# One transformer block on one core: a shared pool of PSUM banks in the projections, a split projection in the last attention unit, and late tokens normalised a step ahead

## The chip, the cores and the metric

The kernel runs on one core of a Trainium2 chip. Its engines are TensorE (PE, with its weight loads shown as PEld), VectorE (DVE), ScalarE (ACT), GpSimd (POOL) and SyncE (SP, which here issues nearly all DMAs). Products land in PSUM, eight banks of 512 fp32 columns on 128 partitions. The metric is the device time of one execution in microseconds, as the median over several runs. Smaller is better.

## What is computed

One pre-norm transformer block on 2048 tokens of width 640, in fp32: attention with 32 heads of 20, then a gated feed-forward part of width 1728.

```python
x = A_x                                            # 1 x 2048 x 640
qkv = (layernorm(x) @ A_wqkv).reshape(B, S, 3, 32, 20)
p = softmax(einsum("bhqd,bhkd->bhqk", q, k) * 20 ** -0.5)
h = x + einsum("bhqk,bhkd->bhqd", p, v).reshape(B, S, D) @ A_wo
z = layernorm(h)
out = h + (silu(z @ B_w_gate) * (z @ B_w_up)) @ B_w_down
```

## The kernel before

All 128-wide operands are split into a high and a low fp32r part, so that a product of two of them is three matmuls (high x high, high x low, low x high). The order of all instructions is written out by hand: each engine runs its own queue in the order in which the program emits it, and waits come from the dependences between tiles.

**First stage: queries, keys and values** (from line 704). The tokens come in four chunks of 512. A chunk is loaded, normalised (`norm`, L714; the normalisation itself is `apply`, L719), turned by TensorE (`flip`, L739, by 64-row halves) and split into `z_hi` and `z_lo`. The list `work` (L888 to 895) holds the projections: 40 *blocks* (128 queries or keys x 512 tokens) and 32 *values* (128 tokens x 320 columns). Each is a *sum* of 15 products of 128 rows; all but the first two blocks run as 30 products of 64 rows, first the 15 of rows 0 to 63 (half 0), then, into the same bank, the 15 of rows 64 to 127 (half 1). Products of different halves can run at the same time in the two halves of the array.

In between, TensorE makes part of the row maxima that the softmax needs later. `max_differences` (L192) is one product in each half for a pair of heads, into two banks: ACT takes a Relu of one half of the columns (L197) and DVE a maximum with the rest (L199). `max_twice` (L205) works in one half of the rows: a first product, whose Relu ACT writes to SBUF (L222), and later a `second` product, with which DVE makes the maximum (L216). The queues `early` (240 entries, groups 1 to 7 and one unit of group 0) and `others` (48 entries of group 0) hold these steps; `next_pair` (L507) takes from one or the other, and a step is usable only when its staged keys and queries have landed and are ready. Keys are staged in places that `raw_place` and `place` (L363 to 372) prepare.

The order is made by a planner that runs while the program is emitted, the class `Halves` (L514, object `pe`). It keeps a model clock for each half (`t`), the time at which each engine is free (`free`, moved by `use`) and the time at which PSUM banks are free. There are two sets of banks: three for sums (`ones`, L525) and five for maxima and turns (`single`, L523). `pair` (L583) issues a step of the maxima if the two oldest of the five banks are free by the model; a `max_twice` takes both of them from its first product on, and its second bank stays marked as taken until `finish_second` (L639) has issued the second product. `run` (L650) starts a sum when one of the three banks is free, and then alternates between the halves by their model clocks; `issue` (L547) emits one product; `may_follow` (L572) says whether half 1 of the oldest sum may run. `before_flip` (L616) waits in model time for two banks. `finish` and `drain` (L674, L681) complete sums and maxima at the end.

PSUM is opened three times: a pool for the first turns (`psum_f`, L70), closed at L869; a second for the rest of the stage (`psum`, L871), closed at L991; and one for attention (`psum_a`, L995: four `ps_one`, three `ps_max`, one `acc`). After attention a fourth (`psum2`, L1494) has four `ps_b` and four `ps_a`.

**Attention** (loop at L1417). 32 units (8 groups of 4 heads x 4 chunks of queries), each with 16 slots, one for 128 keys. In a slot TensorE makes four score products (`scores`, L1331, 62 rows each), ACT four exponentials (L1342), and `weigh` (L1344) multiplies the probabilities of the slot before with the values, in four 32-column tiles, into the bank `acc`. The remaining maxima (`max_one`, L224, and DVE's L235) are placed between the scores by the strings in `ORDER`. Without maxima left the slot is `"sSsSW"`, where W is the weighing and whatever hangs on it: one step from the list `extra`, among others. In the last two units `extra` is the output projection of a finished chunk of tokens (`projection`, L1038): eight steps `first` (`project`, 15 matmuls of 128 rows x 320 columns, L1070, then on DVE the addition L1076 and the statistics L1077), three of normalisation, and four turns (`flip`, L1095), each of which copies and splits its result with `split` (high part by ACT at L88, low part by DVE at L89).

**Feed-forward** (from L1494). The last two chunks are projected, and chunks 2 and 3 are normalised, turned, combined and stored for later in small steps, one in each step of the first products (`late_tokens`, L1831 on: `apply` L1859 makes a normalised tile in one of two buffers, `flip` L1874 turns it with L1878). Then the gate and up products (`ps_a`, L1514), and the down products (`ps_b`, L1608) follow, whose results DVE adds to `h` (L1613); the last row of tokens is stored by L1672.

## Time and profile before

| | us |
|---|---|
| median of 3 runs | 2040.0 |
| lowest and highest of them | 2034.8, 2041.55 |
| the profiled execution, its own time | 2035.66 |
| its span, first to last instruction | 2033.9 |
| mean granted clock of TensorE in it | 0.997 |

The stages, by the trace: the first exponential of attention starts at 328.69, the last unit's slots run from about 1418 to 1468, and the last product ends at 2030.

How to read the rows. In the view of busy time by stretches a row has the stretch, its length, and then for PE, weight load, DVE, ACT and POOL the busy us and, in brackets, the instructions; then the granted clock of TensorE (1.00 is full), the busy share of the DMA engines, and GB/s. A group by line has line, engine, operation, tile written <- tiles read, shapes and count, then busy us and mean ns of one, then the idle time of the engine just before them. In the view of one line the three numbers after a count are the shortest, median and longest duration in ns, and the two after them the first and last start. A row of the timeline has start, duration, engine, line, operation, and in square brackets the idle time before it and what ended it; consecutive equal instructions are merged. A row of the waits has who waited, for whom, us in total, how often, and the longest. The busy time of PE is modelled and overlaps, so the rate at which products start says more than the busy share.

### The profile page before, as it was taken

The page shows a single profiled execution, that of the slowest core. Times are in us where ns is not written, and L with a number is a line of the kernel's source. Part 1 is how long each engine was busy: PE and PEld are TensorE (multiplying, and loading weights), DVE is VectorE, ACT ScalarE, POOL GpSimd, SP SyncE. Part 2 cuts the span into 40 slices and gives each one's busy share as a digit, 9 for nine tenths or more (in the row PEclk, how much of TensorE's full clock was granted, in tenths as well). Part 3 has the DMA queues.
Part 4 walks back from the last instruction along what each step waited for, and adds up shares of the span by engine and source line. Part 5 has one row for each costly group of instructions (what it writes and reads, how often), then busy time and mean ns, then how long its engine had stood idle before and what let it go on. Part 6 is the DMA issues. An engine that isn't in the chain of part 4 may idle for free. (4 is left out here: it accounts for less than half of the span.)

```text
span 2033.9 us, 39129 instructions
## 1 busy us (share of the span) xinstructions
PE 2008.8 (99%) x13716; PEld 1238.9 (61%) x13716; DVE 1612.6 (79%) x3241; ACT 1462.4 (72%) x2952; POOL 785.7 (39%) x1079
## 2 busy tenths in 40 slices
PE   7999999999999999999999999999999999999999
PEld 6899996333333333333333333345598888888888
DVE  6678788888888888888888888885377666676677
ACT  3788988999999999999999999987633222211221
POOL 5554450334434334344430011011145454744555
PEclk9999999999999999999999999999999999999999
DMA  7776663343443534444433123211158654974642
GB/s 227 243 222 186 203 185 100 113 128 99 150 124 113 163 123 138 129 141 146 141 126 109 30 65 80 83 62 49 41 193 292 222 193 156 346 272 159 202 151 95
DMA packets 205124, 305.03 MB, mean 150 GB/s; under 512 B 47664, under 2 KB 82480, under 8 KB 203904
## 3 DMA queue, kind: packets, MB, share of 16 engines
q1 hardware_dynamic: 204832, 302.53, 45.9%
q8 instruction: 109, 1.79, 0.4%
q14 instruction: 87, 0.71, 0.1%
q10 hardware_dynamic: 96, 0.00, 0.0%
HBM read 205.78 MB, written 95.68 MB: 148 GB/s over the span
## 5 line engine op out<-in xcount | busy, mean ns | idle before, releaser
L1342 ACT ACTIVATE probs<-ps_one 128x512 f32<-128x512 f32 x2048 | 1056.9, 615 | 62.0 <-PE ps_one L1336 24.2
L235 DVE TENSOR_REDUCE mx<-ps_max 128x1 f32<-128x512 f32 x1472 | 925.4, 684 | 116.2 <-PE ps_max L229 64.1
L1336 PE MATMUL ps_one<-q_stk,k_stk 62*128 62x512 f32 x2048 | 583.5, 431 | 1.2 <-DVE mx L199 1.2
L1346 PE MATMUL acc<-probs,v_stk 128*32 128x512 f32 x4096 | 546.7, 605 | 0.0
L229 PE MATMUL ps_max<-k_stk,q_stk 60*128 60x512 f32 x1472 | 488.7, 440 | 0.1
L1336 PEld LDWEIGHTS ps_one<-q_stk,k_stk 62*128 62x128 f32 x2048 | 290.5, 185 | 284.7 <-ACT probs L1342 269.7
L229 PEld LDWEIGHTS ps_max<-k_stk,q_stk 60*128 60x128 f32 x1472 | 245.2, 185 | 165.4 <-DVE mx L235 126.9
L1729 DVE TENSOR_TENSOR tmp<-ps_a,tmp 128x512 f32<-128x512 f32 x208 | 141.3, 690 | 122.1 <-PE ps_a L1514 96.4
L1346 PEld LDWEIGHTS acc<-probs,v_stk 128*32 128x32 f32 x4096 | 80.6, 108 | 181.7 <-issue 169.5
L1608 PE MATMUL ps_b<-halves,yp 128*128 128x320 f32 x1032 | 179.0, 308 | 1.5 <-POOL yp L89 1.3
L1608 PEld LDWEIGHTS ps_b<-halves,yp 128*128 128x128 f32 x1032 | 165.2, 188 | 17.5 <-POOL yp L89 1.5
L1514 PE MATMUL ps_a<-t,units 128*128 128x512 f32 x624 | 162.5, 396 | 0.0
L246 POOL CAST both<-neg 128x16 fp32r<-128x16 f32 x32 | 6.6, 207 | 361.6 <-PE ps_one L1336 153.7
L1514 PE MATMUL ps_a<-z,units 128*128 128x512 f32 x516 | 133.9, 394 | 0.0
L89 POOL TENSOR_TENSOR yp<-y,yp 128x256 fp32r<-128x256 f32 x96 | 60.2, 627 | 189.8 <-ACT yp L88 189.8
L1514 PEld LDWEIGHTS ps_a<-t,units 128*128 128x128 f32 x624 | 112.6, 188 | 18.5
L1613 DVE TENSOR_TENSOR h<-ps_b,h 128x320 f32<-128x320 f32 x248 | 110.0, 482 | 6.9 <-PE ps_b L1608 5.4
L216 DVE CUSTOM_DVE_ANT_0 q_stk<-ps_single,q_stk 128x512 f32<-128x512 f32 x143 | 95.7, 689 | 22.4 <-ACT q_stk L222 15.0
L1514 PEld LDWEIGHTS ps_a<-z,units 128*128 128x128 f32 x516 | 93.1, 187 | 16.0
L556 PE MATMUL ps_one<-z_hi,w_hi 64*128 64x512 f32 x380 | 99.1, 402 | 1.8 <-ACT z_hi L88 1.7
L88 ACT ACTIVATE yp<-tmp 128x512 fp32r<-128x512 f32 x40 | 25.3, 632 | 103.2 <-POOL tmp L1601 103.2
L1381 POOL TENSOR_TENSOR o<-o,rb 128x512 f32<-128x512 f32 x31 | 39.9, 1286 | 152.9 <-ACT probs L1342 55.8
(221 smaller groups left out, 3017.9 us busy)
## 6 DMA issues: line engine op xcount, KB each, us to landing
units<-w_d SPq DMA_DIRECT2D x186, 256.0 KB
w_d<-stage SPq DMA_DIRECT2D x106, 256.0 KB
halves<-j_d SPq DMA_DIRECT2D x70, 320.0 KB
k_stk<-qk_d SPq DMA_DIRECT2D x112, 160.0 KB
j_d<-stage SPq DMA_DIRECT2D x42, 320.0 KB
q_stk<-qk_d SPq DMA_DIRECT2D x64, 160.0 KB
k_stk<-qk_d SPq DMA_DIRECT2D x112, 80.0 KB
rb<-r_d SPq DMA_DIRECT2D x32, 256.0 KB
```

The source lines that it names most:

```text
L89: lo_engine.tensor_tensor(out=lo, in0=src, in1=hi.bitcast(F32), op=ALU.subtract)
L216: nc.vector.tensor_tensor_reduce(out=place, in0=pss[1], in1=place, scale=1.0, scalar=LEAST, op0=ALU.add, op1=ALU.max, accum_out=mx[:, b, p ...
L229: nc.tensor.matmul(ps, queries[u][rows, pair, t * P : (t + 1) * P], keys[u // NC][rows, pair, kc * CH : (kc + 1) * CH], start=True, stop=True,
L235: nc.vector.tensor_reduce(mxs[u][:, b, pair, t, kc : kc + 1], ps, axis=AX.X, op=ALU.max)
L556: product = nc.tensor.matmul(job["ps"][:, :out], lhs, rhs, start=(half == 0 and i == 0), stop=(half == 1 and i == job["n"] - 1),)
L1336: nc.tensor.matmul(ps, keys[u // NC][rows, p, kt * P : (kt + 1) * P], queries[u][rows, p, :], start=True, stop=True,)
L1342: nc.scalar.activation(probs[p][:, b, :], ps, AF.Exp, scale=scale)
L1346: nc.tensor.matmul(acc[32 * j : 32 * j + 32, :], values[u // NC][:, kt, j * VW : j * VW + 32], probs[j // 2][:, j % 2, :], start=(kt == 0) ...
L1514: nc.tensor.matmul(ps.rearrange("p (t n) -> p t n", t=TPC), w[k][:, i], z[k][:, :, j], start=(first and m == 0), stop=(last and m == len(n ...
L1608: nc.tensor.matmul(ps, a, b, start=(n == 0), stop=(n == len(pairs) - 1))
L1613: nc.vector.tensor_tensor(out=h, in0=ps, in1=h, op=ALU.add)
L1729: add = lambda out, ps, x: nc.vector.tensor_tensor(out=out, in0=ps, in1=x, op=ALU.add)
```

## The change

**PSUM.** One pool with one tile of eight banks serves the whole kernel. The names `ps_wide`, `ps_one`, `ps_max`, `ps_b` and `bank` now return slices of it by turns. Nothing is closed and opened again. For attention the planner's four oldest banks become `ps_one`, the next three `ps_max`, the last `acc`.

**Planner.** There is one table of eight banks, `places`. `banks(n)` gives the n oldest if they are free by the model. A sum takes one when it starts, and any number of sums may be open. A `max_twice` takes one bank for its first product, and another only when the second product is issued. `others` goes first whenever it holds more than a quarter as many entries as `early`. `before_flip` issues products of half 1 while it waits, and two assertions become `finish_before`, which completes older sums.

```diff
+BEHIND = 2
+SHARE = 4
...
+    psum = ctx.enter_context(tc.tile_pool(name="psum", bufs=1, space=bass.MemoryType.PSUM))
+    banks = psum.tile([P, 8, CH], F32, name="banks")
+    wide_places, one_places = [2, 4, 6], []
+
+    def turn(places):
+
+        places.append(places.pop(0))
+        return places[-1]
...
     def ps_one():
-        return psum.tile([P, CH], F32, name="ps_one", tag="ps_one", bufs=ones)
...
+        return banks[:, turn(one_places) if one_places else pe.take()]
...
-        def second():
-            product(pss[1], first)
+        def second(at):
+            ps, = ps_at(at)
+            product(ps, first)
...
         def next_pair():
             load_items()
-            queues = (others, early) if slot[0] >= begins(NC - 1) else (early, others)
+            first = slot[0] >= begins(NC - 1) or len(others) * SHARE > len(early)
+            queues = (others, early) if first else (early, others)
...
-                self.single = [[0.0] for _ in range(5)]
+                self.places = dict.fromkeys(range(8), 0.0)
...
+            def oldest(self):
+                return sorted(self.places, key=self.places.get)
+
             def banks(self, n):
-                return all(
-                    at[0] is not None and at[0] + MARGIN <= self.now() for at in self.single[:n]
-                )
+                places = self.oldest()[:n]
+                return places if self.places[places[-1]] + MARGIN <= self.now() else None
...
             def pair(self):
                 t = self.now()
-                if not self.banks(2):
+                if not self.banks(1):
                     return False
...
+                at = self.banks(1 if half is not None else 2)
+                if at is None:
+                    return False
+                second = queue.pop(ahead)[1](at)
                 if half is not None:
                     start = self.stream(half, 0.231)
-                    del self.single[:2]
                     seen = self.use("scalar", 0.48, start + 0.43) + 0.2
-                    bank = [None]
-                    self.single += [[seen], bank]
-                    self.second[half] = second, seen, bank
+                    self.places[at[0]] = seen
+                    self.second[half] = second, seen
                     return True
...
+            def finish_before(self, c):
+                while any(job["c"] < c for job in self.jobs):
+                    if self.may_follow():
                         self.issue(1)
                         self.pair()
                     else:
                         self.rest()
+
+            def finish_second(self, half):
+                if not self.second[half]:
+                    return False
+                second, seen = self.second[half]
+                at = self.banks(1)
+                if at is None or self.now() + 0.43 < seen:
+                    return False
+                self.second[half] = None
+                second(at)
+                start = self.stream(half, 0.231)
+                self.places[at[0]] = self.use("vector", 0.62, max(seen, start + 0.43)) + 0.14
+                return True
...
+                while not self.banks(1):
+                    if not self.finish_second(1) and self.may_follow():
+                        self.issue(1)
+                        self.pair()
+                    else:
+                        self.rest()
+                job["place"], = self.banks(1)
+                self.places[job["place"]] = math.inf
...
+    places = pe.oldest()
+    one_places, max_places, acc_place = places[:4], places[4:7], places[7]
```

**Smaller edits of the first stage.** The raw places are filled by an ACT copy instead of two small DMAs; chunk 1 is normalised on DVE instead of POOL, and the planner's price for POOL's goes from 1.3 to 2.55.

```diff
         def raw_place():
-            return place(raw_tile().rearrange("p a b -> p (a b)")[:, : 2 * CH])
...
+            return place(raw_tile().rearrange("p a b -> p (a b)")[:, : 2 * CH], nc.scalar)
...
+            if engine is nc.scalar:
+                some = w_hi.rearrange("p k c -> p (k c)")[:, : 2 * CH].bitcast(F32)
+                nc.scalar.activation(t, some, AF.Copy)
+                pe.use("scalar", 1.0)
+                return t.rearrange("p (h n) -> p h n", h=2)
...
-                (nc.gpsimd if c else nc.vector).tensor_scalar(
+                (nc.gpsimd if c > 1 else nc.vector).tensor_scalar(
...
-                + [(("pool", 1.3), lambda t=t: apply(t), c) for t in range(TPC)]
+                + [
+                    (("pool", 2.55) if c > 1 else ("vector", 0.75), lambda t=t: apply(t), c)
+                    for t in range(TPC)
+                ]
```

**Attention.** The first slot has no maxima. In the last unit W weighs two slots at once in every even slot and none in the odd ones, up to the last. The projection that runs there (of chunk 1) is made in two halves of 64 rows into two banks, the second two products behind the first, and added by two DVE operations; its turns leave the high part to DVE too.

```diff
+            rows = [slice(b * ROW, (b + 1) * ROW) for b in range(2)] if halved else [slice(0, P)]
+            pss = [ps_of() for _ in rows]
+            terms = ((o_hi, wo_hi), (o_hi, wo_lo), (o_lo, wo_hi))
+            for n in range(3 * ND + BEHIND * (len(rows) - 1)):
+                for i, (r, ps) in enumerate(zip(rows, pss)):
+                    m = n - BEHIND * i
+                    if 0 <= m < 3 * ND:
+                        (a, w), k = terms[m // ND], m % ND
+                        nc.tensor.matmul(
+                            ps[:, :HALF], a[r, k, :], w[r, k, hs],
+                            start=(m == 0), stop=(m == 3 * ND - 1),
+                        )
             h = h_c[c][:, t, hs]
-            nc.vector.tensor_tensor(out=h, in0=ps[:, :HALF], in1=h, op=ALU.add)
+            for ps in pss:
+                nc.vector.tensor_tensor(out=h, in0=ps[:, :HALF], in1=h, op=ALU.add)
...
+                if c == 0:
+                    split(src, hi, lo, nc.vector)
+                else:
+                    nc.vector.tensor_copy(hi, src)
+                    nc.vector.tensor_tensor(out=lo, in0=src, in1=hi.bitcast(F32), op=ALU.subtract)
...
-            order = ORDER[now[0] % len(ORDER)] if singles[0] or singles[1] else "sSsSW"
+            order = ORDER[now[0] % len(ORDER)] if now[0] and (singles[0] or singles[1]) else "sSsSW"
...
-                    if todo:
-                        weigh_next()
+                    both = u == NU - 1 and kt < NT - 1
+                    for _ in range(2 * (1 - kt % 2) if both else 1):
+                        if todo:
+                            weigh_next()
```

**Feed-forward.** The late tokens' steps are reordered, so that each tile is normalised a step before it is turned, in five steps for each pair of tiles instead of six; the last row of tokens is stored in two parts.

```diff
+            tt = self.c * TPC + self.t + i
+            first = HALF if tt == NT - 1 else 0
+            if self.fs[0] == NF - 2 and (half == 1 or first):
...
+                cs = slice(first * half, D if half else HALF)
+                nc.sync.dma_start(out[tt * P : (tt + 1) * P, cs], h_c[self.c][:, self.t + i, cs])
...
-        items = moments() + [lambda: apply(2, 0)]
+        items = moments() + [lambda: apply(2, 0), lambda: apply(3, 0)]
         short = len(items)
         items.append(store)
+        items.append(lambda: flip(2, 0))
         for t in range(TPC):
...
+            more = t + 1 < TPC
+            items += [
+                lambda t=t, more=more: (store(), more and apply(2, t + 1), flip(3, t)),
+                lambda t=t, more=more: (store(), sums(t), more and apply(3, t + 1)),
+                lambda t=t, more=more: (store(), more and flip(2, t + 1)),
+                lambda t=t: (store(), keep(zz[2, t], t_d[0], t)),
+                lambda t=t: (store(), keep(zz[3, t], t_d[1], t, nc.vector)),
+            ]
```

171 lines of the change are left out of this document (66 added, 105 removed).

## The prediction

> **What bounds the kernel now.** I read the page first, then busy time by stretches, then the counts by line in the first stage, then the waits and the timeline of the places that the edits touch.
>
> ```profile
> span 2033.9 us, 39129 instructions
> PE 2008.8 (99%) x13716; PEld 1238.9 (61%) x13716; DVE 1612.6 (79%) x3241; ACT 1462.4 (72%) x2952; POOL 785.7 (39%) x1079
> ```
>
> A PE that is 99% busy says little here: in the first 326 us most products use 64 of the 128 rows, and two may run at once, one in each half of the rows. The stretches (time; then busy us and instructions of PE, weight load, DVE, ACT, POOL; granted clock; DMA share; GB/s) show three kinds of stage.
>
> ```profile
> 40.00:80.00 40.00, 36.42 (x336) 33.49 (x335) 18.81 (x79) 25.68 (x67) 24.94 (x17) 0.96 0.73 224
> 49.20:50.80 1.60, 0.03 (x1) 0.00 (x0) 0.00 (x0) 0.00 (x0) 1.60 (x2) 1.00 0.95 223
> 52.40:55.70 3.30, 3.30 (x18) 3.15 (x17) 1.55 (x8) 2.30 (x7) 3.30 (x3) 0.52 0.62 165
> 80.00:320.00 240.00, 238.59 (x2310) 223.04 (x2309) 192.66 (x680) 202.70 (x434) 114.34 (x85) 1.00 0.67 207
> 326.00:328.10 2.10, 0.68 (x2) 0.18 (x1) 2.05 (x12) 1.30 (x5) 0.00 (x0) 1.00 0.48 187
> 328.20:335.70 7.50, 7.50 (x33) 3.29 (x37) 4.92 (x8) 4.93 (x10) 0.00 (x0) 0.54 0.30 92
> 337.00:1360.00 1023.00, 1023.00 (x7190) 401.56 (x7186) 908.75 (x1491) 996.83 (x1968) 313.70 (x526) 1.00 0.36 112
> 1418.00:1452.00 34.00, 34.00 (x227) 21.69 (x219) 10.32 (x28) 20.38 (x40) 5.96 (x4) 1.00 0.19 52
> 1520.00:1560.00 40.00, 37.66 (x199) 32.09 (x198) 30.93 (x62) 16.05 (x33) 22.39 (x21) 1.00 0.80 281
> 1560.00:1760.00 200.00, 200.00 (x1034) 174.18 (x1033) 140.10 (x262) 46.00 (x100) 99.56 (x155) 1.00 0.65 224
> ```
>
> Attention (337 to 1360) is ACT's: 996.83 of 1023 us. The steady feed-forward stage is PE's, without a gap. The change leaves the work of both as it is, so what it can win lies in the first 337 us, in the last unit (1418 to 1470) and around 1520 to 1560.
>
> How full is the first stage? Counts by line, and one price of a stream:
>
> ```profile
> L556 PE MATMUL ps_one<-z_hi,w_hi 64*128 64x512 f32 x380 | 99.1, 402 | 1.8 <-ACT z_hi L88 1.7
> L556 PE MATMUL ps_one<-w_lo,z_hi 64*128 64x320 f32 x320 | 63.4, 308 | 0.0
> L216 DVE DVE_READ_ACCUMULATOR2_ANT mx<- x208: 77/83/88, 133.7 to 321.3; 128x1 f32 x104
> L216 DVE CUSTOM_DVE_ANT_0 q_stk<-ps_single,q_stk x143: 678/691/693, 133.0 to 320.7; 128x512 f32<-128x512 f32 x143
> L199 DVE DVE_READ_ACCUMULATOR2_ANT mx<- x160: 78/83/85, 53.3 to 328.0; 128x1 f32 x160
> 1556.27 2.09 PE ps_a L1514 x9
> 23.97 0.73 PE L556 MATMUL ps_one<-z_hi,w_hi 64*128 64x512 f32 x2
> ```
>
> Nine products of 512 columns in 2.09 us are 0.232 us each; 320 columns are 0.147 (0.73 us for five, in the slot shown below). The sums are three rows like the first (1140 products) and three like the second (960). Each of the 208 accumulator reads of L216 stands for two products, each of the 160 of L199 for one: 576. With both halves always streaming that is (1140 x 0.232 + 960 x 0.147 + 576 x 0.232) / 2 = 270 us; with about 8 for the 120 transposes, 278. It runs from 23.97 to 326: 302 us. **So 24 us, 8%, are lost to one half standing idle, to PE waits and to a halved clock.** That is the most that the edits of this stage can give.
>
> **The change, part by part.**
>
> 1. *Chunk 1 normalised on DVE instead of POOL.*
>
> ```profile
> 39.04 5.00 POOL L720 TENSOR_SCALAR xt<-xt,mv,r_a 128x640 f32<-128x640 f32 x2 [2.05 <-PE ps_one L556]
> 45.27 5.48 POOL L720 TENSOR_SCALAR xt<-xt,mv,r_a 128x640 f32<-128x640 f32 x2
> 50.80 0.27 PE L745 MATMUL ps_single<-ident,xt 64*128 64x64 f32 x2 [1.57 <-POOL xt L720]
> L720 DVE TENSOR_SCALAR xt<-xt,mv,r_a x4: 605/609/611, 11.1 to 12.7; 128x640 f32<-128x640 f32 x4
> ```
>
> Four operations of 2.5 us on POOL end at 50.75; PE's first turn of chunk 1 waits for the last. On DVE they are 4 x 0.61 = 2.4 us, on an engine busy for 18.81 of these 40 us, so the turn finds its input ready. That removes the idle 1.6 us (49.2 to 50.8) and, if the clock is then not halved, half of 3.3 us (52.4 to 55.7): 1.6 + 1.6 = 3.2. What may be late next is the copy and split on ACT, busy 25.68 of 40. The new fill of four raw places (two small DMAs each become one 128x1024 ACT copy; two 512-wide activations of 0.60, L1342's row under part 3, are 1.2 us, 4.8 in all) goes into ACT's 14 idle us there; with that cover gone it costs up to 4.8. The eight DMA issues that go only free SP. I take **-3**, ends -5 and +2.
>
> 2. *One pool of eight banks.* Before, three banks are the sums' and five the pairs' and turns', and a product that has a partner holds two of five from its start. After, any step takes the oldest free bank, a sum may start while a bank is free, and the partner's bank is taken when the partner is issued. No instruction is added to a product. What it can win is the idle half: 24 less the 3.2 of part 1 leaves 21 us. Against all of it speaks ACT, busy 202.70 of 240: were 17 us of that stretch gone it would be at 91%, and its work comes in bursts. The trace has no row for a bank that the planner withheld; the bounds are -17 (all) and +15 (rival D). A quarter, **-4**, is nearest to what ACT leaves between its bursts. The order of the queue (four-to-one between the later groups' products and those of the first) moves products, not their number: 0. The planner's new POOL price of 2.55 matches the rows above; in later chunks no PE wait for POOL's normalisation shows: 0.
>
> 3. *Start of attention.* The scores' first banks now are the four oldest, and the closing of the pool is gone, as are the three maxima of the first slot.
>
> ```profile
> PE ps_one L1336 <- DVE mx L199: 1.2, 1, 1.2
> 328.69 4.03 ACT L1342 ACTIVATE probs<-ps_one 128x512 f32<-128x512 f32 x8 [1.39 <-PE ps_max L229]
> 334.58 0.60 ACT L1342 ACTIVATE probs<-ps_one 128x512 f32<-128x512 f32 x1 [1.86 <-PE ps_one L1336]
> 337.16 2.07 ACT L1342 ACTIVATE probs<-ps_one 128x512 f32<-128x512 f32 x4 [0.18 <-PE ps_max L229]
> ```
>
> PE idles before 328.1 for DVE's last maxima, is then at half clock until 335.7, and ACT loses 1.39 + 1.86 us and some smaller gaps: between 328.69 and 337.16, 8.5 us, it makes twelve exponentials, three slots, worth 3 x 2.07 = 6.2. So 2.3 lie here, plus the 1.2 before it, plus what the earlier start gives. The skipped maxima come back in one slot at the end of their row; a slot with maxima leaves ACT idle for (1023 - 996.83)/1023, under 3% of it: nothing. Ends 0 and -6; **-4**.
>
> 4. *Last unit.* One slot with a projection now:
>
> ```profile
> 1421.03 0.76 PE L1336 MATMUL ps_one<-q_stk,k_stk 62*128 62x512 f32 x4
> 1421.72 1.06 PE L1346 MATMUL acc<-probs,v_stk 128*32 128x512 f32 x8
> 1422.72 1.00 PE L1070 MATMUL ps_max<-wo_hi,o_hi 128*128 128x320 f32 x5
> 1423.56 0.90 PE L1070 MATMUL ps_max<-wo_lo,o_hi 128*128 128x320 f32 x5
> 1424.29 0.90 PE L1070 MATMUL ps_max<-wo_hi,o_lo 128*128 128x320 f32 x5
> 1425.12 0.76 PE L1336 MATMUL ps_one<-q_stk,k_stk 62*128 62x512 f32 x4
> 1425.22 0.49 DVE L1076 TENSOR_TENSOR h<-ps_max,h 128x320 f32<-128x320 f32 x1 [3.06 <-PE ps_max L1070]
> ```
>
> 4.09 us: scores 0.69 (two pairs stream in 0.46, so 0.23 goes at the change to the 32-column form), weighing 1.00, projection 2.40 (2.20 of stream). In halves 15 products become 30 of 64 rows, two at a time, 17 steps with the lag of two: 2.50, up to 0.3 of it beside the scores, which use the same halves. Two weighings together every other slot halve the changes of form. Two slots: 0.69 + 2.0 + 2.50 + 0.46 + 2.50 = 8.15, less up to 0.6 of overlap, against 8.18. Over four such pairs: 0 to -2.4. The second DVE addition (8 more of 0.49 us) lies in DVE's 23 idle us of 34. In slots 8 to 15, two weighings in a row hold back the next scores for 2.0 us, a slot's worth of exponentials (2.07), so ACT may run dry once per pair of slots, by 0 to 0.4: at most +1.6. The turns' high parts move from ACT to DVE; the slot there is ACT's (2.5 us from 1464.28 to 1466.82) and would be DVE's.
>
> ```profile
> 1464.28 2.15 ACT L1342 ACTIVATE probs<-ps_one 128x512 f32<-128x512 f32 x4
> 1466.82 2.22 ACT L1342 ACTIVATE probs<-ps_one 128x512 f32<-128x512 f32 x4
> 1470.88 1.00 PE L1070 MATMUL ps_b<-wo_hi,o_hi 128*128 128x320 f32 x5 [0.74 <-ACT o L1356]
> PE ps_a L1878 <- DVE z L1861: 2.3, 2, 1.2
> ```
>
> Nothing there. I take **-1**, ends -3 and +3. The 0.74 at the hand-over goes, since the next projection's bank no longer waits for the copy of the last sum: **-0.7**.
>
> 5. *Late tokens.* Two turns wait 2.3 us for a normalised tile made in the same step; after, both first tiles are made ahead and each later one a step before its turn, out of the same two buffers. A buffer is free only when the turn before it has run, so a little may stay: **-2**, ends -2.3 and +1. The last row's store in two parts changes what follows the last addition by one half-width store: 0 within 0.5.
>
> Sum: -3 - 4 - 4 - 1 - 0.7 - 2 = **-14.7**. From the profiled execution's 2035.66 us (span 2033.9) that is 2021; the median of the three runs shown, 2040, lies 4.3 above that execution, and the same step from it gives **2025**.
>
> The clock is told by the rows: 1.6 us with PE idle are followed, 1.6 us later, by 3.3 us at 0.52. The Trainium skill (TensorE: Matmul & The Clock Gate, Why this matters for your kernels) would have only gaps of more than about 3 us do that. The trace does not agree. By the page, closing gaps this short would leave the halved stretches where they are, and the sum would be that of rival C.
>
> **The rivals.**
>
> A. As summed: 2025 (2016 to 2033, parts 2 and 3 between their ends).
>
> B. *The pool gives nothing:* the halves idle for order, or for ACT and DVE, not for banks. For it: ACT is 84% busy from 80 to 320, and PE's largest recorded wait for a bank there is small:
>
> ```profile
> PEld ps_single L210 <- DVE mx L216: 3.2, 11, 0.7
> ```
> Against it: only 5 of the 24 us are PE idle (40 - 36.42 and 240 - 238.59); the rest shows no wait, which is what a step that the planner withheld leaves. Parts 2 at 0 and 3 at -2: 2031.
>
> C. *The clock halves anyway* after the first stage: another short gap of PE, at 326 or at 50, has the same effect. Part 1 loses 1.6 and part 3 all but 1: 2040 - 10 = 2030. For it: any PE gap of 1.6 us did it.
>
> D. *Slower: left-over maxima.* Sums may now hold as many banks as they like until their second half is done, and crowd out the products. What isn't issued by the last sum is drained alone, one at a time through DVE: 0.69 (L216) + 0.08 us each. From 19 left over the 14.7 are gone; 30 give 2040 - 14.7 + 23 = 2048. For it: the old limit of three sums kept five banks for products. Against: 208 + 160 are spread evenly now, and the new order brings the first group's forward.
>
> E. *It evens out:* waits of the in-order PE queue move to other places, 2040.
>
> **Chances.** A 0.52, B 0.17, C 0.10, D 0.13, E 0.08. The range must take in all but 2 in 10: 2010 (A with most of part 2) to 2044 (into D); A's own is 2016 to 2033. A measurement tells 0.3%, 6 us, from no change: faster is A, most of B and C: 0.75; same, E and the edges of B, C and D: 0.13; slower 0.12.
>
> **What would show it.** Part 1: no PE wait for L720 and a clock of 1.00 from 49 to 57. Part 2: the first exponential before 322 us. Part 3: clock 1.00 in the 8 us after it and no gap of ACT over 1 us. Part 4: slots of under 4.0 us with a projection. Part 5: no PE wait for L1861. It would be wrong if the first exponential came later than 328, if new half-clock stretches stood in the first 320 us, or if DVE's maxima ran alone at the end of the stage.

## The result, and the profile after

| | before | after |
|---|---|---|
| median (13 runs each, same chip) | 2038.7 us | 2037.77 us |
| lowest and highest | 2032.58, 2041.94 | 2035.7, 2040.99 |
| profiled execution, own time | 2035.66 | 2040.81 |

The ratio of the times is 0.9998, with a 95% interval of [0.9989, 1.0008]: no change. On 2038.7 us that is -0.4 us [-2.2, +1.6]; forecast was -14.7. The two profiles lie on opposite sides: before's is 3 us under its median, after's 3 us above. So each kernel was profiled once more, and the stages are compared by both profiles. The stages are cut at the exponentials (first start; end of the 64th; starts of the first of unit 30 and of unit 31, and of the first of slot 8 and the last of slot 15), at the last copy of a sum out of `acc`, at the last product and at the last instruction.

| stage, us | before | before again | after | after again | mean change |
|---|---|---|---|---|---|
| up to the first exponential | 328.7 | 334.7 | 335.5 | 332.9 | +2.5 |
| first 64 exponentials | 36.2 | 36.1 | 33.9 | 33.8 | -2.3 |
| attention up to unit 30 | 995.2 | 995.2 | 995.2 | 995.2 | 0.0 |
| unit 30 | 57.4 | 57.5 | 58.3 | 58.2 | +0.8 |
| last unit, slots 0 to 7 | 32.7 | 32.7 | 29.9 | 29.9 | -2.8 |
| last unit, slots 8 to 15 | 18.1 | 18.1 | 22.0 | 20.3 | +3.1 |
| to the last copy of `acc` | 2.0 | 2.0 | 1.8 | 1.8 | -0.2 |
| feed-forward, to the last product | 559.8 | 560.1 | 557.3 | 557.6 | -2.5 |
| to the end | 3.9 | 3.9 | 5.2 | 5.0 | +1.2 |

So the edits did act; gains of 7.8 us stand against losses of 7.6. The page of after:

```profile
span 2039.0 us, 39356 instructions
PE 2009.1 (99%) x13836; PEld 1244.3 (61%) x13836; DVE 1616.7 (79%) x3261; ACT 1463.3 (72%) x2948; POOL 778.5 (38%) x1075
```

Busy time by stretches of after, columns as before; the last three rows are the place of a stall, the start of attention, and a part of slots 8 to 15 of the last unit:

```profile
40.00:80.00 40.00, 36.29 (x318) 33.01 (x316) 22.80 (x102) 30.98 (x81) 17.79 (x13) 0.91 0.76 238
80.00:320.00 240.00, 232.05 (x2196) 215.98 (x2194) 188.65 (x674) 198.84 (x425) 112.66 (x83) 0.99 0.63 194
172.00:177.00 5.00, 4.14 (x23) 3.88 (x25) 4.53 (x18) 2.85 (x6) 0.00 (x0) 0.66 0.22 82
335.50:343.50 8.00, 7.41 (x48) 2.97 (x49) 5.55 (x9) 7.91 (x17) 6.72 (x2) 1.00 0.44 137
1462.50:1467.00 4.50, 4.50 (x23) 1.60 (x22) 0.00 (x0) 2.54 (x5) 1.54 (x1) 0.62 0.02 4
```

In 80 to 320 PE has 8.0 us idle where it had 1.4 in before (8.2 and 1.9 in the second profiles). The waits of PE in the first stage of after say at what:

```profile
PE banks L217 <- ACT q_stk L231: 4.3, 5, 1.6
PE banks L783 <- DVE mx L207: 1.7, 1, 1.7
PE banks L194 <- DMA q_stk<-qk_d: 1.3, 2, 1.0
PE banks L217 <- ACT v_stk L231: 1.2, 1, 1.2
```

The wait for POOL's normalised tile (1.6) is gone; in its place stand waits for a bank that ACT's Relu (L231) or DVE's maximum (L207) still reads, from products that were issued before their bank was free. One of them, in the timelines of PE and then of ACT in after:

```profile
170.79 0.45 PE L569 MATMUL banks<-w_hi,z_lo 64*128 64x320 f32 x2
172.86 0.50 PE L217 MATMUL banks<-raw 60*128 60x512 f32 x1 [1.62 <-ACT q_stk L231]
172.87 0.61 PE L569 MATMUL banks<-w_hi,z_lo 64*128 64x320 f32 x2
```

```profile
169.63 0.60 ACT L231 ACTIVATE v_stk<-banks 128x512 f32<-128x512 f32 x1 [0.39 <-PE banks L217]
172.21 1.21 ACT L231 ACTIVATE q_stk<-banks 128x512 f32<-128x512 f32 x2 [1.98 <-DVE mx L224]
```

DVE is late, so ACT has no place for its Relu, so PE's product has no bank. The running sum, whose bank is open, stands behind that product in PE's queue: it stops with it and goes on 0.01 us after it. The clock then is at 0.66 in 172 to 177. The half-clock stretches of before (52 to 56, 328 to 336) are gone from their places and stand in others. The first of them belongs to one of before's two executions only, as the next section shows.

### The profile page after: what moved, and what is told of

It is laid out like the page before. It is cut to its first block, busy times and chain, and to the rows that moved or that the text cites. A ratio compares the mean times of both kernels' runs of the same rounds, so it can differ in the third digit from the quotient of the medians.

```text
span 2039.0 us, 39356 instructions
## 1 busy us (share of the span) xinstructions
PE 2009.1 (99%) x13836; PEld 1244.3 (61%) x13836; DVE 1616.7 (79%) x3261; ACT 1463.3 (72%) x2948; POOL 778.5 (38%) x1075
## 4 chain that ended last, share of the span: by engine, by line
PE 94%; DMA 2%; DVE 1%; ACT 1%; POOL 1%; issue 1%; SPq 0%; DVEq 0%; ACTq 0%; POOLq 0%
PE banks L1384 25%; PE banks L1374 17%; PE banks L1552 16%; PE banks L238 12%; PE banks L1646 8%; PE banks L569 8%; PE banks L1103 3%; PE banks L217 3%; PE banks L194 1%; DMA qk_d<-e 0%; PE banks L826 0%; PE banks L263 0%; DMA q_stk<-qk_d 0%; ACT q_stk L231 0%; DMA xt<-in_A_x 0%
## 5 line engine op out<-in xcount | busy, mean ns | idle before, releaser
L1380 ACT ACTIVATE probs<-banks 128x512 f32<-128x512 f32 x2048 | 1056.2, 614 | 61.1 <-PE banks L1374 25.3
L244 DVE TENSOR_REDUCE mx<-banks 128x1 f32<-128x512 f32 x1472 | 925.4, 684 | 124.9 <-PE banks L238 76.3
L1374 PE MATMUL banks<-q_stk,k_stk 62*128 62x512 f32 x2048 | 583.2, 428 | 1.5 <-ACT probs L1380 1.5
L1384 PE MATMUL banks<-probs,v_stk 128*32 128x512 f32 x4096 | 545.4, 606 | 0.0
L238 PE MATMUL banks<-k_stk,q_stk 60*128 60x512 f32 x1472 | 486.7, 438 | 0.2
L1374 PEld LDWEIGHTS banks<-q_stk,k_stk 62*128 62x128 f32 x2048 | 291.8, 184 | 283.7 <-ACT probs L1380 271.4
L238 PEld LDWEIGHTS banks<-k_stk,q_stk 60*128 60x128 f32 x1472 | 244.2, 184 | 163.1 <-DVE mx L244 126.8
L1646 PE MATMUL banks<-halves,yp 128*128 128x320 f32 x1032 | 178.9, 308 | 1.4 <-POOL yp L97 1.2
L1646 PEld LDWEIGHTS banks<-halves,yp 128*128 128x128 f32 x1032 | 165.2, 188 | 17.4 <-POOL yp L97 1.5
L1552 PE MATMUL banks<-t,units 128*128 128x512 f32 x624 | 162.7, 396 | 0.1
```

Source lines behind the costliest of these rows:

```text
L238: nc.tensor.matmul(ps, queries[u][rows, pair, t * P : (t + 1) * P], keys[u // NC][rows, pair, kc * CH : (kc + 1) * CH], start=True, stop=True,
L244: nc.vector.tensor_reduce(mxs[u][:, b, pair, t, kc : kc + 1], ps, axis=AX.X, op=ALU.max)
L1374: nc.tensor.matmul(ps, keys[u // NC][rows, p, kt * P : (kt + 1) * P], queries[u][rows, p, :], start=True, stop=True,)
L1380: nc.scalar.activation(probs[p][:, b, :], ps, AF.Exp, scale=scale)
L1384: nc.tensor.matmul(acc[32 * j : 32 * j + 32, :], values[u // NC][:, kt, j * VW : j * VW + 32], probs[j // 2][:, j % 2, :], start=(kt == 0) ...
L1552: nc.tensor.matmul(ps.rearrange("p (t n) -> p t n", t=TPC), w[k][:, i], z[k][:, :, j], start=(first and m == 0), stop=(last and m == len(n ...
```

## Experiments

Ratios are to the kernel before, run on the same chip in between, with 95% intervals; 0.001 is 2.0 us. Groups of runs were on different chips, so only ratios are compared between them. All variants start from the kernel after. Where the text says that products of the maxima stand *behind the last sum*, that is counted in the emitted order.

**Is the difference of the first stage real?** Both kernels unchanged, once more.

> The kernel before once more, for a second profile of it. Theory V (the first stage varies from execution to execution, because short waits of PE fall differently and a halved clock follows some of them): the first exponential, 328.7 us in the first profile, moves by 2 us or more, while the stretches after it repeat within 0.5 us: 1460.4 to 1460.6 from first to 16th-last... in numbers, last unit's slots 0 to 7 (first exponential to that of slot 8) 32.7 us, slots 8 to 15 18.1 us. Rival F (the first stage is fixed by the program): the first exponential stays within 1 us of 328.7.

> The changed kernel once more, for a second profile. Theory V: the first exponential, 335.5 us in the first profile, moves by 2 us or more, downwards, since that profile's time (2040.81) was the second highest of 13 runs. Rival F: it stays within 1 us of 335.5. Both: slots 0 to 7 of the last unit 29.9 us, slots 8 to 15 21.9 us, as in the first profile.

Measured: 0.9997 [0.9987, 1.0007] and 1.0003 [0.9991, 1.0014]. The first exponential of *before* came at 334.7 this time and that of *after* at 332.9: both moved by more than 2 us, as theory V has it. The two stretches of before from 40 to 80:

```profile
40.00:80.00 40.00, 36.42 (x336) 33.49 (x335) 18.81 (x79) 25.68 (x67) 24.94 (x17) 0.96 0.73 224
```

```profile
40.00:80.00 40.00, 32.67 (x298) 29.21 (x296) 14.64 (x60) 22.89 (x58) 25.39 (x16) 0.96 0.68 200
```

The same program issued 38 products fewer. The forecast's "24 us lost" was read off an early execution of a stage that scatters by some 6 us. The second profile of before also has PE's wait of 1.6 us for POOL, on which part 1 of the prediction rests:

```profile
PE ps_single L745 <- POOL xt L720: 1.6, 1, 1.6
48.00:52.00 4.00, 2.64 (x28) 2.47 (x24) 1.47 (x2) 1.04 (x2) 4.00 (x2) 1.00 0.39 121
52.00:56.00 4.00, 3.77 (x32) 3.56 (x34) 0.86 (x5) 3.35 (x9) 4.00 (x4) 1.00 0.80 210
```

Here the clock stays at 1.00 behind it. So the half clock that followed in the first profile is not a fixed cost of that wait.

**Which part costs?** The first stage alone (all edits of slot 0, of the last unit, of the late tokens and of the last store undone); and all of it, with paired weighing only up to slot 8:

```diff
-                    both = u == NU - 1 and kt < NT - 1
+                    both = u == NU - 1 and kt < 9
```

> The shared pool, the planner, chunk 1 on DVE and the ACT fills alone; the first slot with maxima, the last unit, the late tokens and the last store as before. By the two profiles the other edits of the change sum to +0.9 - 2.8 + 3.8 - 2.4 + 1.2 = +0.7 us after the first 64 exponentials and up to -2.3 before. Theory V (the first stage is even on the whole): ratio to the kernel before between 0.999 and 1.001. Rival F (the first stage lost the 6.8 us that the two profiles show): 1.003.

> The changed kernel with two weighings together only while the projection runs (slots 0 to 8 of the last unit), one in each slot after that. Theory W (two weighings in a row keep the next scores from ACT in slots 8 to 15): these slots go from 21.9 back to about 18 us, slots 0 to 7 stay at 29.9, and the ratio to the kernel before is about 0.998. Rival (the turns on DVE are what makes these slots long): they stay above 20.5 us.

Measured: 1.0004 [0.9995, 1.0013] and 0.9978 [0.9970, 0.9987]. Slots 8 to 15 fall from 22.0 and 20.3 to 17.8 us. What they did in after, by the timelines of PE and of ACT:

```profile
1461.04 1.96 PE L1374 MATMUL banks<-q_stk,k_stk 62*128 62x512 f32 x4 [0.45 <-ACT probs L1380]
1462.93 3.17 PE L1384 MATMUL banks<-probs,v_stk 128*32 128x512 f32 x16
1466.03 1.16 PE L1135 MATMUL banks<-ident,z 128*128 128x128 f32 x5
1467.12 0.73 PE L1374 MATMUL banks<-q_stk,k_stk 62*128 62x512 f32 x4
```

```profile
1455.47 4.03 ACT L1380 ACTIVATE probs<-banks 128x512 f32<-128x512 f32 x8 [0.64 <-PE banks L1374]
1460.39 4.03 ACT L1380 ACTIVATE probs<-banks 128x512 f32<-128x512 f32 x8 [0.90 <-PE banks L1374]
1467.65 4.03 ACT L1380 ACTIVATE probs<-banks 128x512 f32<-128x512 f32 x8 [2.62 <-PE banks L1374]
```

Two weighings in a row take 1.92 us at full clock. After PE's wait of 0.45 the clock is halved, they take 3.17, the turns follow in the same slot, and ACT waits 2.62 us for scores. In the second profile of after the clock is 1.00 throughout these slots, and ACT still waits, for up to 1.6 us; its stretch and two rows of its ACT:

```profile
1450.00:1470.00 20.00, 18.95 (x118) 6.64 (x115) 10.50 (x30) 15.83 (x32) 1.55 (x1) 1.00 0.05 14
1463.30 4.03 ACT L1380 ACTIVATE probs<-banks 128x512 f32<-128x512 f32 x8 [0.99 <-PE banks L1374]
1468.92 2.06 ACT L1380 ACTIVATE probs<-banks 128x512 f32<-128x512 f32 x4 [1.60 <-PE banks L1374]
```

So against 17.8 us the pairs cost 2.6 at full clock, and one halved stretch adds 1.6.

**The small edits of the first stage, one at a time**, on top of the last: the raw places filled by DMA again; chunk 1 back on POOL; the old order of the queues.

```diff
-            return place(raw_tile().rearrange("p a b -> p (a b)")[:, : 2 * CH], nc.scalar)
+            return place(raw_tile().rearrange("p a b -> p (a b)")[:, : 2 * CH])
...
-                (nc.gpsimd if c > 1 else nc.vector).tensor_scalar(
+                (nc.gpsimd if c else nc.vector).tensor_scalar(
...
-            first = slot[0] >= begins(NC - 1) or len(others) * SHARE > len(early)
+            first = slot[0] >= begins(NC - 1)
```

> As e4, but the raw places are filled by two small DMAs each again. e4 measured 0.9978. Theory A (three ACT fills in a row, 2.93 us from 56.56 in the first profile of the change, hold back the Relus, hence DVE's maxima, hence the next turn: PE waits 1.65 us for DVE, and half a clock follows): no PE wait of a turn for DVE near 60 us, no half clock there, the first exponential 2 to 3 us earlier, ratio 0.9963 to 0.9968. Rival (the fills cost nothing that another wait would not cost): 0.9973 to 0.9983.

> As e4, but chunk 1 is normalised on POOL again, with the planner's price at 2.55. Theory P (chunk 1 on DVE is worth the 3 us that the prediction gave it): ratio 0.9990 to 0.9995, and a wait of PE for L755 in the trace. Rival (the 3 us are lost again to the next waits of the same stretch): 0.9973 to 0.9983.

> As e4, with the old order of the two queues of maxima (the first group's last, until the last chunk). Theory O (the order moves products and not their number, worth nothing): 0.9973 to 0.9983. Rival (the new order brings the first group's keys back early, so that attention can start sooner): the first exponential at least 2 us later than in e4's profile (330.7), ratio above 0.9988.

Measured: 1.0000 [0.9991, 1.0009], 0.9973 [0.9963, 0.9982], 0.9987 [0.9978, 0.9996], beside 0.9978. The ACT copies do not cost time: without them it is slower, which neither theory A nor its rival expected. (Part of that may be the DMAs themselves: PE's waits for them are 4.8 us in that run's list of longest waits, 0.4 with the copies. That they are the cause is not shown.) The old queue order differs by less than the intervals can tell. Chunk 1 on DVE is worth nothing, though its stall is gone. The stretches with it on DVE (first fence), and on POOL (second):

```profile
40.00:80.00 40.00, 37.27 (x353) 34.14 (x350) 25.38 (x117) 33.52 (x88) 18.95 (x14) 1.00 0.81 257
80.00:320.00 240.00, 233.65 (x2223) 215.91 (x2221) 188.38 (x677) 199.81 (x429) 112.46 (x83) 0.99 0.63 196
```

```profile
40.00:80.00 40.00, 36.73 (x313) 32.36 (x311) 18.05 (x84) 29.35 (x74) 26.10 (x16) 0.96 0.78 240
80.00:320.00 240.00, 237.99 (x2267) 221.51 (x2265) 196.25 (x712) 203.19 (x444) 112.50 (x83) 1.00 0.64 199
```

On DVE 40 products more are done by 80 us, and 44 fewer from there to 320: 2576 against 2580. The lead is given back in full. DVE and ACT, too, have done the same by 320 in both (794 and 796 instructions on DVE, 517 and 518 on ACT), as they would if they set the pace; no run tests that. Where it is given back, the rows do show: with chunk 1 on DVE, PE is idle for 6.4 us of 80 to 320, with it on POOL for 2.0. But the pool alone, with chunk 1 on POOL (next), has 6.3, so this edit is not the only one that brings such waits.

**The pool and nothing else.** All other edits undone.

> The changed kernel with only the pool of eight banks and its planner left: the four raw places filled by DMA, chunk 1 normalised on POOL, the planner's price of POOL at 1.3, the groups' queues in their old order, and all edits of the last unit, of slot 0 and of the late tokens undone. Theory B (the pool gives nothing in the first stage; the hand-over of banks gives 2.3 us at the start of attention): ratio 0.9985 to 0.9995, first exponential within 328 to 336. The forecast's own term (-4 for the pool, -4 for the start): 0.996. Theory L (the pool by itself loses 2 to 4 us, since sums hold banks until their second half is done): 1.000 to 1.001, first exponential after 333.

Measured: 0.9984 [0.9975, 0.9994], first exponential at 331.0, first 64 exponentials in 33.9 us. That is -3.3 us [-5.1, -1.2], of which 2.3 lie at the start of attention. What the small edits add to it is a loss: the first stage with all of them had 1.0004, and the intervals are just apart. The profiles of the two differ by 5.3 us, of which 3.7 lie in the first stage and 1.3 at the very end. Undoing the small edits one at a time, above, doesn't give this back, so it can't be put on one of the three.

**Does the late second bank matter?** With chunk 1 on POOL (0.9973), a `max_twice` takes both its banks at its first product again, out of the eight.

```diff
-                at = self.banks(1 if half is not None else 2)
+                at = self.banks(2)
...
+                    self.places[at[1]] = math.inf
```

> Paired weighing in slots 0 to 7 only, chunk 1 on POOL, and a max_twice again takes both its banks, from the one pool of eight, at its first product. Theory B (late taking of the second bank gives nothing): ratio 0.9965 to 0.9982, as with the late one (0.9973). If the late second bank carries the gain that the forecast gave the pool (4 us), 0.999 to 1.000. If holding the second bank too crowds out the products so that they are left over and drained at half clock, as at the margin of 0.8: over 1.002, with the first exponential after 340.

Measured: 0.9991 [0.9980, 1.0001], first exponential 332.6, first 64 exponentials 35.8. Here 32 products of the maxima stand behind the last sum, in before 6, in after none. So the late bank is worth some 3.7 us (0.0018; the two intervals just overlap): it lets all maxima be issued ahead of the last sum, and two of the 3.7 are again the start of attention.

**Does skipping the maxima of slot 0 help?** They are put back (paired weighing to slot 8, chunk 1 on POOL).

```diff
-            order = ORDER[now[0] % len(ORDER)] if now[0] and (singles[0] or singles[1]) else "sSsSW"
+            order = ORDER[now[0] % len(ORDER)] if singles[0] or singles[1] else "sSsSW"
```

> The changed kernel with paired weighing in slots 0 to 7 only, chunk 1 on POOL and the maxima of slot 0 back. If skipping those maxima wins nothing at the start and costs 0.8 us in unit 30, as the traces have it, unit 30 falls from 58.3 to 57.5 us, the first 64 exponentials stay at 34 us, and the ratio is 0.9969 beside 0.9973 with the maxima skipped. If skipping them is what shortened the start, the first 64 exponentials go back to 36 us and the ratio is 0.998.

Measured: 0.9969 [0.9957, 0.9981]; unit 30 in 57.6 us, the first 64 exponentials in 33.9. The skipping only moved 0.8 us into unit 30.

**Are the waits a matter of the planner's margin?** 0.8 us (on the kernel of 0.9978) and 0.0 (on that of 0.9973) instead of 0.2.

```diff
-MARGIN = 0.2
+MARGIN = 0.8
```

> As e4, with the planner's margin on a bank at 0.8 us instead of 0.2. Theory M (the pool hands out a bank by a model in which ACT is done sooner than it is; PE, in order, then stands before a product for up to 1.6 us, 5.5 us in all in the first profile of the change): the PE waits of L217 for ACT fall below 1.5 us in sum, 80 to 320 us has PE busy above 237 of 240, first exponential 2 to 4 us earlier, ratio 0.9958 to 0.9968. Rival (a bank withheld is as bad as a bank waited for): 0.9973 to 0.9990.

> Paired weighing in slots 0 to 7 only, chunk 1 on POOL, and the planner's margin for a free bank 0.0 instead of 0.2 us. Theory W (withheld banks are what the planner loses, as the margin of 0.8 showed): fewer banks withheld, first exponential 1 to 4 us earlier, ratio 0.9955 to 0.997 beside 0.9973 at 0.2. Theory I (the waits of the in-order queue, each with its half clock, are the price of issuing on time): PE waits for banks grow by some us and the ratio is 0.998 to 1.000.

Measured: 1.0100 [1.0085, 1.0116] and 1.0029 [1.0019, 1.0039]. At 0.8, 132 products of the maxima stand behind the last sum; stretches and timeline of that run:

```profile
80.00:320.00 240.00, 232.93 (x2210) 215.82 (x2208) 165.46 (x588) 179.84 (x390) 109.88 (x82) 0.97 0.64 196
320.00:352.00 32.00, 31.89 (x93) 17.10 (x92) 29.73 (x103) 27.47 (x53) 3.79 (x3) 0.50 0.25 72
```

```profile
334.78 0.79 PE L217 MATMUL banks<-raw 60*128 60x512 f32 x1
335.39 0.86 PE L217 MATMUL banks<-xt,raw 60*128 60x512 f32 x2
336.21 0.79 PE L217 MATMUL banks<-raw 60*128 60x512 f32 x2
336.82 0.80 PE L217 MATMUL banks<-xt,raw 60*128 60x512 f32 x2
```

DVE does 165 us of work from 80 to 320 instead of 188, and the rest is drained alone: four products in each 1.42 us, at half clock, to 352. This is rival D's mechanism, brought on by hand; in the change itself it did not occur. At 0.0 nothing is left behind, and the first exponential still comes at 342.2, 11.4 us later than at 0.2. PE's listed waits grow by 3.4 us only (5.3 to 8.7), so issuing yet earlier into banks that are not free explains a part; the rest is not explained.

**Between the two.** With slot 0's maxima back, chunk 1 on POOL and paired weighing to slot 8 (0.9969), margins of 0.4 and 0.6, which leave nothing behind the last sum; then the planner's prices of ACT and DVE half way to those of the trace, which shows 0.596 and 0.687 (and 0.08 for the accumulator read) where the planner has 0.48 and 0.62:

```profile
L231 ACT ACTIVATE q_stk<-banks 128x512 f32<-128x512 f32 x124 | 71.5, 596 | 16.8 <-DVE mx L224 7.0 <-PE banks L569 4.6 <-PE banks L217 3.8
L224 DVE CUSTOM_DVE_ANT_0 q_stk<-banks,q_stk 128x512 f32<-128x512 f32 x124 | 82.8, 687 | 24.1 <-PE banks L217 11.5 <-PE banks L569 8.2 <-ACT q_stk L231 3.7
```

```diff
-MARGIN = 0.2
+MARGIN = 0.4
...
-                    seen = self.use("scalar", 0.48, start + 0.43) + 0.2
+                    seen = self.use("scalar", 0.54, start + 0.43) + 0.2
```

> Paired weighing in slots 0 to 7 only, chunk 1 on POOL, maxima of slot 0 back (0.9969 with the margin of 0.2), and the planner's margin at 0.4 us; in the emitted order all 576 products of the maxima still stand ahead of the last sum (at 0.8 us, 132 stood behind it). Theory Q (the planner prices ACT and DVE too low, 0.48 and 0.62 us against 0.60 and 0.77 in the trace, so it issues into banks that are not free yet, and the in-order queue stalls both halves): fewer PE waits, first exponential 2 to 6 us sooner than 328.2, ratio 0.994 to 0.996. Theory O (at 0.8 the sums ran ahead only because the maxima were left behind): 0.9965 to 0.999.

> As before with the margin at 0.6 us; nothing is left behind the last sum either. Theory Q: first exponential at 318 to 324, ratio 0.992 to 0.995. Theory O: 0.997 to 1.001.

> As before with the margin of 0.2 us, but the planner's prices half way to the measured ones: 0.54 for the Relu of 512 columns, 0.69 for the maximum over them, 0.34 and 0.43 for 256 columns (0.48, 0.62, 0.3, 0.36 before). Nothing is left behind the last sum. Theory Q: ratio 0.994 to 0.9965, PE waits for L231 and L224 shrink. Theory O: 0.9965 to 0.999.

> The margin at 0.4 us, with chunk 1 normalised on DVE as in the change; paired weighing in slots 0 to 7 only, maxima of slot 0 back. If the 3 us that chunk 1 on DVE wins in 40 to 80 us are lost again in waits behind it, and the longer margin removes those waits, this is 1 to 3 us below the same with chunk 1 on POOL. If the lead is worth nothing because ACT and DVE set the pace behind it, both are equal within 0.001.

> The same fastest kernel with the margin at 0.3 us, between 0.2 (0.9969) and 0.4 (0.9943); nothing is left behind the last sum. If the time follows the margin smoothly, the ratio is 0.995 to 0.9965. If each value only deals another order of the first stage, with another set of stalls, it may lie anywhere from 0.994 to 1.000, and one outside 0.9945 to 0.997 says so.

Measured, in this order: 0.9943 [0.9932, 0.9955], 0.9994 [0.9983, 1.0005], 0.9969 [0.9957, 0.9981], 0.9956 [0.9945, 0.9968], 0.9980 [0.9972, 0.9989]. Over margins of 0.2, 0.3, 0.4 and 0.6 that is 0.9969, 0.9980, 0.9943, 0.9994: no trend. Theory Q met its ratio at 0.4 alone, and there the waits of PE were not shorter (7.5 us listed, 5.9 at 0.2), nor was the first exponential of the profile earlier (328.2 in both). From the waits at 0.4:

```profile
PE banks L569 <- ACT z_hi L96: 2.7, 4, 0.9
PE banks L783 <- ACT v_stk L351: 1.6, 1, 1.6
PE banks L569 <- ACT q_stk L231: 1.4, 2, 0.9
```

Theory Q falls as a rule. Theory O doesn't stand either, since 0.9943 lies outside its range. Every edit of the planner deals a new order of the whole stage with stalls in other places, worth some thousandths up or down. Chunk 1 on DVE again gave nothing (0.9956 against 0.9943, intervals overlapping).

**Halved projection or paired weighing?** The kernel of 0.9943 with no paired weighing.

```diff
-                    both = u == NU - 1 and kt < 9
+                    both = False
```

> The fastest so far (margin 0.4, paired weighing in slots 0 to 7 only, chunk 1 on POOL, maxima of slot 0 back: 0.9943) with no paired weighing at all. If the halved projection alone makes slots 0 to 7 shorter (32.7 to 30.0 us), they stay below 30.5 and the ratio at 0.994 to 0.995. If weighing two slots at once is what shortens them, they go to 31.5 to 32.7 us and the ratio to 0.995 to 0.9958.

Measured: 0.9951 [0.9938, 0.9965]. Slots 0 to 7 take 30.9 us (30.0 with it), slots 8 to 15 17.0 (17.8 with it). Over all sixteen the two are equal, 47.9 and 47.8, against 50.8 in before: the halved projection (-1.8 in slots 0 to 7), with the turns' high parts on DVE (-1.0 in slots 8 to 15), carries the gain, and paired weighing only moves time between slots. The slot as it is in this run:

```profile
1421.61 0.63 PE L1374 MATMUL banks<-q_stk,k_stk 62*128 62x512 f32 x4
1422.18 1.07 PE L1384 MATMUL banks<-probs,v_stk 128*32 128x512 f32 x8
1423.17 1.03 PE L1103 MATMUL banks<-wo_hi,o_hi 64*128 64x320 f32 x10
1424.03 0.90 PE L1103 MATMUL banks<-wo_lo,o_hi 64*128 64x320 f32 x10
1424.76 0.90 PE L1103 MATMUL banks<-wo_hi,o_lo 64*128 64x320 f32 x10
1425.50 0.63 PE L1374 MATMUL banks<-q_stk,k_stk 62*128 62x512 f32 x4
```

It is 3.89 us long, against 4.09. This run has the same first stage as that at the margin of 0.4 and repeats its time on another chip, so that order is truly the better one: 10 to 12 us below both kernels (0.9951 and 0.9943 of 2038 us).

## Why the prediction was wrong

The time lay in the range (2010 to 2044), but only because the range is wide: a gain was forecast with 0.75, and there was none. By the two profiles of each kernel, 9.5 of the 14.5 us that are missing lie in the first stage, where -3 and -4 were forecast and the stage came 2.5 later. By its steps:

1. *Chunk 1 on DVE, -3:* **failed**. The stall for POOL was read rightly and is gone. But a turn's wait of 1.7 us stands between 54 and 61 instead, for DVE, which waits for ACT, where three of the new fills run for 2.93 us: the delay on ACT that the step named and left out of its sum. The other half of the 3.2, for the halved clock, rested on one execution: the second profile of before has the stall without it. Above all, the step priced a local stall as if the stage were a chain. Of the products that came earlier, all 40 were given back by 320. With the pool's order the stall also goes without this edit: with chunk 1 on POOL no PE wait for POOL shows, and with the pool alone one of 0.5 us. What in the order gives the lead back was not isolated.
2. *Pool, -4:* mis-sized; alone, about -1 in the stage and -2.3 at the start of attention. Nothing near the bound of 21 us was found: the earliest first exponential of all twenty profiles is at 327.6, 1.1 before that of before. That no wait showed for the halves' idle time was taken as a sign of withheld banks; the late second bank may gain a little (0.0018, with intervals that just overlap), but withholding fewer still (margin 0.0) made it slower by 0.0056. The fills, "up to +4.8", were wrongly sized too: undoing them made it slower by 0.0022. Queue order "0" is not refuted: undoing it made it slower by 0.0009, with overlapping intervals. The new POOL price was not undone by itself.
3. *Start of attention, -4:* mechanism right, size -2.3. After has no maxima left at the end, the clock is 1.00 in 335.5 to 343.5 and ACT runs without a gap of 1 us. All twenty profiles agree: the first 64 exponentials take 35.4 to 36.2 us in the six that have a half clock there, and 33.8 to 34.2 in the other fourteen. The 1.2 us of idle PE that were counted besides did not come off, since the stage then ends with its sums: the last ones stream at full rate to 334.8. Skipping the maxima was put at nothing and cost 0.8.
4. *Last unit, -1, and hand-over, -0.7:* slots 0 to 7 gave -2.8 (0 to -2.4 forecast), of which the halved projection alone -1.8. The turns' high parts, put at nothing, gave about -1. Paired weighing in slots 8 to 15 **failed**: with it they took 20.3 and 22.0 us, without it 17.0, where "at most +1.6" was forecast. The sum let ACT run dry by 0 to 0.4 us for each pair. At full clock it ran dry by 0.6 to 0.9 behind a pair alone and by 1.0 to 1.6 where a turn follows the pair, which the sum did not count; in one of the two profiles a halved clock came on top. Of the hand-over's 0.7 a wait of 0.4 for POOL remains.
5. *Late tokens, -2:* right. The feed-forward stage is 2.5 us shorter with the hand-over in it; in the two runs with the late tokens as before (first stage only, pool alone) it is some 0.6 shorter, so about -2 is theirs. No PE wait for L1861's counterpart is left; what PE waits for from 1470 to 1570 in after is this alone:

```profile
PE banks L1103 <- POOL o_lo L97: 0.4, 1, 0.4
```

The last store, "0 within 0.5": the end came 1.2 us later, but it did also in the first-stage run with one whole store, and not in the run of the pool alone, also with one. So the two-part store is not shown to be the cause. It stays open.

Of the rivals, E (2040, the waits move) has the time and the mechanism, at a chance of 0.08. Part of the balance is chance, though: gains in attention and feed-forward happen to equal losses of other edits. B was half right about the pool. C happened as an addition: the clock halves at other places. Its support, that any gap of 1.6 us halves the clock, does not hold (last section).

Open remains which property of the order of the first stage sets its time; margins and prices did not show it. The half clock by itself doesn't: with chunk 1 on DVE and a margin of 0.4 it never was halved there and the first exponential came at 327.8; in the run without paired weighing it was halved twice, and it came at 327.6.

## What to carry to other kernels

Before a stage's lost time is counted as winnable, profile the unchanged kernel twice: here two executions differed by 6 us in the stage at stake, more than any single edit gave. In a stage whose order a model emits, price an edit by what has been done at the end of the stage and not at the stall removed. Measure it with each edit undone as well, since any edit reshuffles the order, which here moved the time by some thousandths. Before two long operations are put in a row in front of the engine that sets the pace, look at what else follows them in the same slot: here the pairs cost 2.6 us at full clock, and 4.2 where the clock was halved.

## What was not expected of the hardware

The same order of instructions can get a different clock. The run with paired weighing to slot 8 and the kernel after are alike up to the last unit; both have a gap of PE of 0.59 us just after the first exponential. In the former, where that starts at 330.69, the clock then fell, as its stretch shows:

```profile
334.00:338.00 4.00, 4.00 (x21) 1.49 (x19) 1.89 (x3) 2.88 (x6) 3.44 (x1) 0.61 0.54 151
```

In after, where it starts at 335.51, it stayed at 1.00 (the stretch 335.5 to 343.5 above). The former needed 35.4 us for the 64 exponentials, the latter 33.9. The first stage of after ran in four profiles (after, after again, first stage only, paired weighing to slot 8). All four have a PE gap of 1.6 to 1.7 us between 54 and 61; the clock fell behind it in the first two and stayed at 1.00 in the others.

Counted over all twenty traces, PE has 55 gaps of 1 us or more between 20 and 345. A half clock began within 2.3 us of the end of 24 of them: of all six above 2 us, and of 18 of the 49 shorter ones. Every stretch at half clock that the traces record before the end of the last product lasts 3.41 us or a whole multiple of it (6.83, 13.65 and 51.2 occur). One of 3.41 us therefore costs PE at most 1.7 us of work.

Gaps of 0.45 to 2.8 us were followed by a halved clock in some executions, which the Trainium skill (TensorE: Matmul & The Clock Gate, Why this matters for your kernels) has only for gaps of more than about 3 us. These traces do not agree, and it makes part of the scatter. A PE that the profile shows busy can be at half clock for long as well: 0.50 over the 32 us of the drain above.
